# Talking-heads attention with a gated layer: value products two chunks in a run at a slot's end, and loads of q, k, v and of the first weights begun from ScalarE's queue

## The chip, the core and the metric

The kernel runs on one core of one Trainium2 chip. The metric is device time in microseconds (us), the median of several executions of one launch. TensorE (PE) multiplies into PSUM banks, with weight loads shown apart as PEld; VectorE (DVE), ScalarE (ACT) and GpSimd (POOL) do the elementwise work; transfers are begun by SyncE (SP) or by ACT, which each have a queue of their own, and are carried by 16 DMA engines that both queues share. Each engine works off its own instructions in the order in which they are written; an instruction that has to wait holds up all behind it on that engine.

## The reference, cut to what matters

```python
# 4 batches, 12 heads, 448 positions, 64 wide; 1792 tokens of 768
scores = scale * np.matmul(q, k.transpose(0, 1, 3, 2))
scores = np.einsum('bhij,hg->bgij', scores, w_pre)        # heads mixed before the softmax
scores = scores - np.max(scores, axis=-1, keepdims=True)
attn = np.exp(scores)
attn = attn / (np.sum(attn, axis=-1, keepdims=True) + 1e-09)
attn = np.einsum('bhij,hg->bgij', attn, w_post)           # and after it
attn_out = np.matmul(attn, v)
x = attn_out.transpose(0, 2, 1, 3).reshape(B * S, H * D)
gate = 1.0 / (1.0 + np.exp(-(x @ w_gate)))
out = gate * (x @ w_val) @ w_out
```

## The kernel before

The attention part works in 16 blocks of query rows (per batch 120, 120, 120 and 88 rows), cut into 180 groups of 10 rows. Ten rows times twelve heads fill the 120 partitions of one tile, so that one product mixes the heads. Slots t, one per group, set the order: the loop `for t in range(...)` writes one slot after the other, and each engine's share of a slot follows its share of the slot before.

In slot t stand, for different groups and blocks: `qk` (L163, L164), the scores of one head of the block after next or so, which `keep` copies to a tile `st` (L172 on ACT for odd heads, L174 on DVE for even ones); `premix(t + 4)` (L203), the first mix of heads, from the tile `T` into one of two PSUM banks `pm`; `rowmax(t + 4)` (L210, DVE); `p_lo(t + 1)` (L248, DVE) and `scale(t + 2)` (L233, POOL); `mix(t - 1)` (L266, ACT); what the plan holds for the slot (loads, splits of k and q on POOL, `av`); `expo(t + 4)` (L219, ACT), which frees a `pm` bank; the slot's share of the second part (`moe.slot`); and `postmix(t)` (L260), the second mix, twelve short products `mx`.

`regroup(t)` (L198) moves ten rows of `st` to one of five tiles `T`, from SP, written up to seven slots ahead; it waits until `premix` of five groups earlier has read that tile, and, for the first group of a block, until all twelve heads of the block are in `st`. There are two tiles `st`, so the first copy of a block into `st` waits until the last `T` of the block before the last has landed.

`av(bi, c)` (L280) multiplies values: chunk c of six of block bi is 16 short products. After chunk 3 and after chunk 5 ACT copies the result (`xt`, L288) and begins its store (`xs`, L289). The six chunks of a block were spread over the slots of the next block by `at(spread(c, KC, s0, s1), av, bi, c)`.

All loads are written by `nc.sync.dma_start`, in the slots that `fit(loads)` gives them: 18 of k (L122, 448 KB each), 15 of q (L140, 528 or 720 KB), 12 of v (L181, 512 KB). They stand on SP between the transfers of `T`. The second part (`_Moe`) has a plan of its own, made ahead of time; its weights are loaded raw (L839, 768 KB each), turned into float32 on ACT and DVE (L848, L852, L857), stored (L861) and loaded again (L864); its first weights and the rows of x (L872) are loaded in the last slots of the attention.

The DMAs of the two queues take eight semaphores, named DMAHW0 to DMAHW7 in the listings below, in turn: each DMA first waits for the landing of the one written eight DMAs before it, where that is not yet known.

Of the kernel before, what the change touches and what calls it, by code (L numbers as in the profile page):

```python
# [14 lines left out]
I8 = mybir.dt.int8  # L15
# [19 lines left out]
def _attention(ctx, tc, ins, B, H, S, D, xs, raws, make_moe):  # L35

    nc = tc.nc
    qd, qp, kd, kp, vb = (ins[n] for n in ("qd", "qp", "kd", "kp", "vb"))
# [3 lines left out]
    KC = H * D // 128  # L42
# [29 lines left out]
    def bank(pool, tag):  # L72
        return pool.tile([128, 512], F32, tag=tag, name=tag)
# [35 lines left out]
    NG = len(groups)  # L109
    moe = make_moe(NG)  # L110
# [8 lines left out]

    def k_load(b, c):  # L120
        t = kld[len(kraw) % len(kld)]
        nc.sync.dma_start(out=t, in_=kd[b, c])  # L122
        kraw[b, c] = t

    def k_split(b, c, e):
# [10 lines left out]
    def q_load(bi):  # L136

        b, i0, n, _ = blocks[bi]
        t = qld.tile([128, H * QB], F32, tag="qd", name="qd")
        nc.sync.dma_start(out=t[:, :H * n], in_=qd[b, :, H * i0:H * (i0 + n)])  # L140
        qraw[bi] = t[:, :H * n].rearrange("p (h s) -> p h s", s=n)

    def q_split(bi, u):
# [34 lines left out]

    def v_load(b, u):
        t = vst.tile([128, QUAD, 4, D], F32, tag="v", name="v")  # L180
        nc.sync.dma_start(out=t.rearrange("p h j d -> p (h j d)"), in_=vb[b, u])  # L181
        vt[b, u] = t


# [6 lines left out]
    def pairs(t):  # L191

        return kind[t]

    def regroup(t):
        _, bi, r0 = groups[t]
        T = tp.tile([KR, S], F32, tag="T", name="T")
        nc.sync.dma_start(out=T, in_=st_t[bi][r0:r0 + R])  # L198
        t_t[t] = T

    def premix(t):
        ps = bank(ps_pm, "pm")
        nc.tensor.matmul(ps[:, :S], lhsT=w1, rhs=t_t.pop(t), start=True, stop=True)  # L203
        sc_t[t] = ps

    def rowmax(t):

        nm = sm.tile([128, 1], F32, tag="nm", name="nm")
        junk = jp.tile([128, S], F16, tag="junk", name="junk")
        nc.vector.tensor_scalar(junk, sc_t[t][:, :S], -SCALE, None, op0=ALU.mult, op1=ALU.min,  # L210
                                accum_out=nm)
        nm_t[t] = nm

    def expo(t):
        e = ep.tile([128, S], F32, tag="e", name="e")
        if t % 2 == 0:
            ss_p[0] = sm.tile([128, 2], F32, tag="ss", name="ss")
        ss = ss_p[0][:, t % 2:t % 2 + 1]
        nc.scalar.activation(out=e, in_=sc_t.pop(t)[:, :S], func=AF.Exp, bias=nm_t.pop(t),  # L219
                             scale=SCALE, accum_out=ss)  # L220
        e_t[t], ss_t[t] = e, ss

    def norm():
        nc.vector.tensor_scalar(ss_p[0], ss_p[0], 1e-9, 1.0 / P_UP, op0=ALU.add, op1=ALU.mult)

    def recip():
        nc.vector.reciprocal(ss_p[0], ss_p[0])

    def scale(t):

        if pairs(t):
            ph = pp.tile([128, S], F16, tag="ph", name="ph")
            nc.gpsimd.tensor_scalar(ph, e_t[t], ss_t[t], 1.0, op0=ALU.mult, op1=ALU.mult)  # L233
            p_t[t] = [ph]
            if pairs(t) == 2:
                e, pl = e_t.pop(t), pp.tile([128, S], F16, tag="pl", name="pl")
                nc.gpsimd.tensor_scalar(e, e, ss_t.pop(t), 1.0, op0=ALU.mult, op1=ALU.mult)
                nc.gpsimd.tensor_tensor(pl, e, ph, op=ALU.subtract)
                p_t[t].append(pl)
        else:  # L240
            w = wp.tile([128, H * R], F32, tag="w2s", name="w2s")
            nc.gpsimd.tensor_scalar(w, w2, ss_t.pop(t), 1.0, op0=ALU.mult, op1=ALU.mult)
            p_t[t] = w

    def p_lo(t):
        if pairs(t) == 1:
            pl = pp.tile([128, S], F16, tag="pl", name="pl")
            nc.vector.scalar_tensor_tensor(pl, e_t.pop(t), ss_t.pop(t), p_t[t][0], op0=ALU.mult, op1=ALU.subtract)  # L248
            p_t[t].append(pl)

    def postmix(t):
        ps = bank(ps_mx, "mx")[:, :4 * H * R].rearrange("p (j c) -> p j c", j=4)
        if pairs(t):
            ph, pl = p_t.pop(t)
            terms = [(ph, w2hi), (ph, w2lo), (pl, w2hi)]
        else:
            terms = [(e_t.pop(t), p_t.pop(t))]
        for jb in range(4):
            for i, (a, w) in enumerate(terms):
                nc.tensor.matmul(ps[:, jb, :], lhsT=a[:, JB[jb]:JB[jb] + 128], rhs=w,  # L260
                                 start=(i == 0), stop=(i == len(terms) - 1))
        mx_t[t] = ps

    def mix(t):
        _, bi, r0 = groups[t]
        nc.scalar.activation(out=mixes[bi % 2][:, :, :, r0:r0 + R],  # L266
                             in_=mx_t.pop(t).rearrange("p j (g r) -> p j g r", r=R), func=AF.Copy, scale=fm)
# [25 lines left out]
    SOFT = 4  # L293
# [5 lines left out]
    def at(slot, fn, *args):  # L299
        plan.setdefault(slot, []).append((fn, args))  # L300

    def spread(i, n, s0, s1):
        return s0 + i * (s1 - s0) // n
# [38 lines left out]
    for bi in range(1, NBK):  # L342
        s0, s1 = qwin[bi]
        for g in range(H):
            at(spread(g, H, s0, s1), qk, bi, g)
        for u in range(NQ):
            due = spread(u * QUAD, H, s0, s1) - 2
            if bi > 1:
                splits.append((due - 4 if u else due - 2, due, q_split, bi, u))
        if bi > 1:  # L350
            loads.append((max(s0 - 12, -5), max(s0 - 8, -1), q_load, bi))
    fit(loads)
    fit(splits, lambda slot: slot % 4)
    for bi in range(NBK):
        s0 = first[bi + 1] + 1
        s1 = first[bi + 2] + 1 if bi + 2 < len(first) else s0
        for c in range(KC):
            at(spread(c, KC, s0, s1), av, bi, c)
            if bi == NBK - 1:
                at(s1, moe.between, c)  # L360

# [25 lines left out]
    def qk_first(g, pool, tag):  # L387
        n = blocks[0][2]
        c, e = divmod(g, 2)
        sc = bank(pool, tag)  # L390
        nc.tensor.matmul(sc[:n, :S], lhsT=qraw[0][HI[e], c], rhs=kone[0, c][HI[e]], start=True, stop=True)
        return sc
# [13 lines left out]
    for c in range(1, NP):  # L406
        k_first(c)
    mix_in = load_mix()
    q_load(1)
    hb = bank(ps_av, "av")  # L410
    warm(10)
# [3 lines left out]
    todo = [qk_first(g, *pools[g]) for g in range(AHEAD)]  # L415
# [18 lines left out]
    for t in range(min(min(plan), -LEAD), max(plan) + 1):  # L434
        while next_dma < min(NG, t + LEAD + 1) and t >= qwin[groups[next_dma][1]][1]:
            regroup(next_dma)
            next_dma += 1
        todo = plan.get(t, ())
        for fn, args in todo:
            if fn is qk:  # L440
                fn(*args)
        if 0 <= t + SOFT < NG:
            premix(t + SOFT)
            rowmax(t + SOFT)
        sums = t % 2 == 0 and 0 <= t + PREP < NG + 1
        if sums:
            norm()
        if 0 <= t + 1 < NG:
            p_lo(t + 1)
        if sums:  # L450
            recip()
        if 0 <= t + 2 < NG:
            scale(t + 2)
        for c in hooks.get(t, ()):
            c.close()
        if 0 <= t - 1 < NG:
            mix(t - 1)
        for fn, args in todo:
            if fn is not qk:
                fn(*args)  # L460
        if 0 <= t + SOFT < NG:
            expo(t + SOFT)
        if t == NG:
            nc.scalar.activation(out=iw, in_=sw, func=AF.Sigmoid)
        moe.slot(t)
        if 0 <= t < NG:
            postmix(t)
    return moe


# [19 lines left out]
class _Moe:  # L490
# [345 lines left out]

    def load_raw(self, k):

        self.nc.sync.dma_start(out=self.at["raw", k].bitcast(I8)[:, :8 * self.WE - 3], in_=self.src[k].bitcast(I8)[:, 3:])  # L839

    def top(self, k, step):

# [77 lines left out]

    def slot(self, t):
        a = t - self.NG
        if a == self.ROOM[0][0]:
            self.open(0)
        if a == self.ROOM[1][0]:
            self.open(1)
        if a == 0:
            self.open(2)
        if a == -3:
            self.open_banks(5, side="right")  # L930
        self.until(min(self.SLOT * (a + 1), 3.4) if a else 3.4)
# [98 lines left out]
```

## Time and profile before

| | |
|---|---|
| median of 3 runs | 1010.58 us (1008.87 to 1017.09) |
| the profiled execution, its own time | 1007.51 us |
| its span, first to last instruction | 1005.6 us |
| attention, about | 0 to 510 us of the span |
| PE busy | 939.6 us (93%) |
| DVE, ACT, POOL busy | 696.9, 613.1, 275.7 us |
| mean granted TensorE clock | 0.981 of full speed |
| chain that ended last | PE 63%, DMA 17%, ACT 11%, DVE 5% |
| bytes moved by the DMA engines | 144.48 MB |

A row of a timeline gives the start in us from the span's start, the duration in us, the engine (with a q where only its queue is at work), line, operation and tiles; in square brackets stands how long the engine had been idle before, and what ended that.

### The profile page before, as it was taken

The page shows a single profiled execution, that of the slowest core. Times are in us where ns is not written, and L with a number is a line of the kernel's source. Part 1 is how long each engine was busy: PE and PEld are TensorE (multiplying, and loading weights), DVE is VectorE, ACT ScalarE, POOL GpSimd, SP SyncE. Part 2 cuts the span into 40 slices and gives each one's busy share as a digit, 9 for nine tenths or more (in the row PEclk, how much of TensorE's full clock was granted, in tenths as well). Part 3 has the DMA queues.
Part 4 walks back from the last instruction along what each step waited for, and adds up shares of the span by engine and source line. Part 5 has one row for each costly group of instructions (what it writes and reads, how often), then busy time and mean ns, then how long its engine had stood idle before and what let it go on. Part 6 is the DMA issues. An engine that isn't in the chain of part 4 may idle for free.

```text
span 1005.6 us, 17847 instructions
## 1 busy us (share of the span) xinstructions
PE 939.6 (93%) x6606; PEld 749.7 (75%) x6606; DVE 696.9 (69%) x1243; ACT 613.1 (61%) x1061; POOL 275.7 (27%) x354
## 2 busy tenths in 40 slices
PE   7889999899989999979789999999899999999998
PEld 2656676566766677656568888888699999999997
DVE  7556777578665667645468877788988766669882
ACT  3555667566665666667596888799455444446460
POOL 6246755478546864422210000000000000000000
PEclk8899999999999999999999999999899999999999
DMA  5666567665677665766825555778644321210002
GB/s 162 158 165 171 133 129 190 156 169 114 146 195 173 139 125 118 176 164 133 237 90 185 192 189 188 250 242 292 207 146 166 94 63 52 75 48 1 28 10 74
DMA packets 71333, 144.48 MB, mean 144 GB/s; under 512 B 18167, under 2 KB 49999, under 8 KB 71247
## 3 DMA queue, kind: packets, MB, share of 16 engines
q1 hardware_dynamic: 58024, 137.63, 50.0%
q10 hardware_dynamic: 13223, 5.70, 2.1%
q8 instruction: 53, 0.87, 0.3%
q14 instruction: 33, 0.27, 0.1%
HBM read 79.44 MB, written 25.17 MB: 104 GB/s over the span
## 4 chain that ended last, share of the span: by engine, by line
PE 63%; DMA 17%; ACT 11%; DVE 5%; issue 3%; SPq 1%; ACTq 0%; DVEq 0%
PE bank L888 18%; DMA T<-st 13%; PE bank L899 13%; PE pm L203 11%; PE mx L260 9%; PE av L280 6%; DMA raws<-in_w_dram 4%; ACT raws L852 4%; PE qk L163 3%; ACT m_GV L875 3%; PE qk L164 2%; ACT raws L848 2%; ACT m_FWTR L905 1%; DVE st L174 1%; DVE m_FWTR L881 1%
## 5 line engine op out<-in xcount | busy, mean ns | idle before, releaser
L888 PE MATMUL bank<-m_GV 128*128 128x448 f32 x1512 | 314.2, 368 | 10.8 <-ACT m_FWTR L905 5.2
L888 PEld LDWEIGHTS bank<-m_GV 128*128 128x128 f32 x1512 | 284.1, 189 | 40.0 <-ACT m_FWTR L905 7.8
L210 DVE TENSOR_SCALAR_CACHE_REDUCE junk<-pm 128x448 f16<-128x448 f32 x180 | 112.0, 622 | 132.5 <-PE pm L203 129.1
L203 PE MATMUL pm<-T,w 120*128 120x448 f32 x360 | 173.2, 563 | 28.7 <-DMA T<-st 19.8
L219 ACT ACTIVATE e<-pm,nm 128x448 f32<-128x448 f32 x180 | 114.3, 635 | 124.7 <-DVE junk L210 71.9
L878 DVE TENSOR_TENSOR m_GV<-m_FWTR,m_GV 128x768 fp32r<-128x768 f32 (+1 forms) x137 | 154.4, 1138 | 49.9 <-ACT m_GV L875 47.9
L875 ACT CAST m_GV<-m_FWTR 128x768 fp32r<-128x768 f32 (+1 forms) x137 | 134.9, 1001 | 56.7 <-DVE m_FWTR L881 28.3
L899 PE MATMUL bank<-m_GV 128*128 128x448 f32 x756 | 158.9, 371 | 6.5 <-ACT m_GV L875 3.9
L899 PEld LDWEIGHTS bank<-m_GV 128*128 128x128 f32 x756 | 143.8, 191 | 21.2 <-ACT m_GV L875 4.7
L233 POOL TENSOR_SCALAR ph<-e,ss 128x448 f16<-128x448 f32 x151 | 98.5, 660 | 156.4 <-ACT e L219 94.8
L260 PEld LDWEIGHTS <-ph 128*128 128x128 f16 x1208 | 91.6, 98 | 47.4 <-issue 38.7
L248 DVE SCALAR_TENSOR_TENSOR pl<-e,ss,ph 128x448 f16<-128x448 f32 x151 | 122.2, 809 | 4.1 <-POOL ph L233 3.8
L266 ACT ACTIVATE mix<-mx,fm 128x480 f32<-128x480 f32 x180 | 121.2, 673 | 2.5 <-PE mx L260 2.5
L280 PEld LDWEIGHTS av<-mix,v 128*64 128x64 f32 x1504 | 73.6, 138 | 59.1 <-issue 40.5
L260 PE MATMUL mx<-w2hi,pl 128*128 128x120 f16 x604 | 105.2, 217 | 9.5 <-DVE pl L248 9.5
L260 PE MATMUL mx<-w2hi,ph 128*128 128x120 f16 x604 | 106.3, 219 | 1.5 <-POOL qhh L149 0.6
L260 PE MATMUL mx<-w2lo,ph 128*128 128x120 f16 x604 | 105.3, 217 | 0.0
L203 PEld LDWEIGHTS pm<-T,w 120*128 120x128 f32 x360 | 66.4, 194 | 46.7 <-ACT mix L266 15.7
L280 PE MATMUL av<-mix,v 128*64 128x120 f32 (+1 forms) x1504 | 93.5, 268 | 0.0
L905 ACT COPY m_FWTR<-bank 128x448 f32<-128x448 f32 x96 | 52.8, 554 | 60.4 <-PE bank L888 45.4
L163 PE MATMUL qk<-kT,qhh 128*120 128x448 f32 (+1 forms) x180 | 80.1, 445 | 2.4 <-POOL qhh L149 1.9
L174 DVE COPY st<-qk 120x448 f32<-120x448 f32 (+1 forms) x92 | 56.3, 613 | 35.4 <-PE qk L164 14.6
(70 smaller groups left out, 1041.6 us busy)
## 6 DMA issues: line engine op xcount, KB each, us to landing
T<-st SPq DMA_DIRECT2D x180, 210.0 KB
raws<-in_w_dram SPq DMA_DIRECT2D x36, 767.6 KB
w<-m_FWTR SPq DMA_DIRECT2D x36, 384.0 KB
m_FWTR<-w SPq DMA_DIRECT2D x31, 384.0 KB
raws<-in_kd_dram SPq DMA_DIRECT2D x18, 448.0 KB
qd<-in_qd_dram SPq DMA_DIRECT2D x11, 720.0 KB
raws<-w SPq DMA_DIRECT2D x17, 384.0 KB
v<-in_vb_dram SPq DMA_DIRECT2D x12, 512.0 KB
```

What stands on the lines that cost most here:

```text
L163: nc.tensor.matmul(sc[:n, :S], lhsT=hh[:, h, :n], rhs=kt, start=True, stop=False)
L203: nc.tensor.matmul(ps[:, :S], lhsT=w1, rhs=t_t.pop(t), start=True, stop=True)
L210: nc.vector.tensor_scalar(junk, sc_t[t][:, :S], -SCALE, None, op0=ALU.mult, op1=ALU.min, accum_out=nm)
L219: nc.scalar.activation(out=e, in_=sc_t.pop(t)[:, :S], func=AF.Exp, bias=nm_t.pop(t), scale=SCALE, accum_out=ss)
L248: nc.vector.scalar_tensor_tensor(pl, e_t.pop(t), ss_t.pop(t), p_t[t][0], op0=ALU.mult, op1=ALU.subtract)
L260: nc.tensor.matmul(ps[:, jb, :], lhsT=a[:, JB[jb]:JB[jb] + 128], rhs=w, start=(i == 0), stop=(i == len(terms) - 1))
L266: nc.scalar.activation(out=mixes[bi % 2][:, :, :, r0:r0 + R], in_=mx_t.pop(t).rearrange("p j (g r) -> p j g r", r=R), func=AF.Copy, scale=fm)
L280: nc.tensor.matmul(av_t[bi][64 * i:64 * i + 64, c % 4, :n], lhsT=vt[b, u][:, h + i, jb, :], rhs=mixes[bi % 2][:, jb, 2 * c + i, :n], start ...
L875: self.nc.scalar.copy(self.f32(hi).bitcast(F32R), self.f32(f))
L878: self.nc.vector.tensor_tensor(self.f32(lo).bitcast(F32R), self.f32(f), self.f32(hi), op=ALU.subtract)
L888: self.nc.tensor.matmul(self.f32(bank), lhsT=w[a][:, k], rhs=x[b][:, k], start=self.START[i] and k == r == 0, stop=k == self.KH - 1 and r ...
L899: self.nc.tensor.matmul(self.f32(bank), lhsT=w[a][:, k], rhs=b[bb], start=self.START[i] and j == k == r == 0, stop=j == OUT_TILES - 1 and ...
```

## The change

The loads of k, q and v go from SP's to ACT's queue, and so do raw weight loads up to seven slots before the last group. In a slot `premix` and `rowmax` now stand ahead of `qk`. The chunks of `av` fall due in pairs (chunks 0 and 1, 2 and 3, 4 and 5 in the same slot, every fourth slot of a block of twelve), and they stand at the slot's end, behind `postmix`, with the copy and the store of their result. The last block's six chunks stay together behind the last group.

```diff
     def k_load(b, c):
-        nc.sync.dma_start(out=t, in_=kd[b, c])
+        nc.scalar.dma_start(out=t, in_=kd[b, c])
     def q_load(bi):
-        nc.sync.dma_start(out=t[:, :H * n], in_=qd[b, :, H * i0:H * (i0 + n)])
+        nc.scalar.dma_start(out=t[:, :H * n], in_=qd[b, :, H * i0:H * (i0 + n)])
     def v_load(b, u):
-        nc.sync.dma_start(out=t.rearrange("p h j d -> p (h j d)"), in_=vb[b, u])
+        nc.scalar.dma_start(out=t.rearrange("p h j d -> p (h j d)"), in_=vb[b, u])
...
-            at(spread(c, KC, s0, s1), av, bi, c)
+            at(spread(c - c % 2, KC, s0, s1), av, bi, c)
...
+        if 0 <= t + SOFT < NG:
+            premix(t + SOFT)
+            rowmax(t + SOFT)
         for fn, args in todo:
             if fn is qk:
                 fn(*args)
-        if 0 <= t + SOFT < NG:
-            premix(t + SOFT)
-            rowmax(t + SOFT)
...
+        tail = (av, moe.between)
         for fn, args in todo:
-            if fn is not qk:
+            if fn is not qk and fn not in tail:
                 fn(*args)
         if 0 <= t + SOFT < NG:
             expo(t + SOFT)
+        if t >= NG:
+            for fn, args in todo:
+                if fn in tail:
+                    fn(*args)
...
         if 0 <= t < NG:
             postmix(t)
+            for fn, args in todo:
+                if fn in tail:
+                    fn(*args)
...
     def load_raw(self, k):
-        self.nc.sync.dma_start(...)
+        self.loads.dma_start(...)
...
     def slot(self, t):
         a = t - self.NG
+        self.loads = self.nc.scalar if a < -7 else self.nc.sync
```

On SP, in the first block's slots, the transfers of `T` stood between loads of k (`raws<-in_kd_dram`), q and v before the change:

```order
L198 DMA T<-st 120x1x448 x8
L122 DMA raws<-in_kd_dram 128x896
L198 DMA T<-st 120x1x448
L122 DMA raws<-in_kd_dram 128x896
L198 DMA T<-st 120x1x448
L140 DMA qd<-in_qd_dram 128x1056
L198 DMA T<-st 120x1x448
L181 DMA v<-in_vb_dram 128x1024
L198 DMA T<-st 120x1x448
```

After the change 173 transfers of `T` stand on SP without a load between them, and only the loads of x (`m_FWTR<-xs`, now L880) still stand between the last seven:

```order
L375 DMA mix_132<-in_kp_dram 128x448 x5
L198 DMA T<-st 120x1x448 x173
L880 DMA m_FWTR<-xs 128x3x224 x2
L198 DMA T<-st 120x1x448
L880 DMA m_FWTR<-xs 128x3x224 x2
```

On ACT those loads (49 of them in the slots and ahead of them: 15 of q, 18 of k, 12 of v, 4 of weights) now stand between `mix` and `expo` of a slot; here with what each instruction waits for, in the first block's slots:

```order
L266 ACTIVATE mix_131<-mx,fm 128x48x10
L122 DMA raws<-in_kd_dram 128x896 [waits DMAHW2_49]
L219 ACTIVATE e,ss<-pm,nm 128x448 [waits DVE_49,Activation_49]
L266 ACTIVATE mix_131<-mx,fm 128x48x10 [waits PE_49]
L140 DMA qd<-in_qd_dram 128x1056 [waits DMAHW5_49,Pool_49]
L219 ACTIVATE e,ss<-pm,nm 128x448 [waits DVE_49,Activation_49]
```

A load on ACT waits for one of the eight DMA semaphores, and one of q for POOL as well; the exponentials stand behind it.

On PE a slot with one chunk of `av` read so before the change (an `av` row of x8 is one chunk):

```order
L260 MATMUL mx<-w2hi,pl 128x120
L163 MATMUL qk<-kT,qhh 88x448
L164 MATMUL qk<-kT,qll 88x448
L203 MATMUL pm<-T,w_121 128x448
L280 MATMUL av<-mix_132,v 64x120 x8
L260 LDWEIGHTS ph
L260 MATMUL mx<-w2hi,ph 128x120
```

and after it two chunks stand behind the slot's `mx`, with `premix` of the next slot behind them:

```order
L260 MATMUL mx<-w2hi,pl 128x120
L280 MATMUL av<-mix_131,v 64x120 x16
L203 MATMUL pm<-T,w_121 128x448
L163 MATMUL qk<-kT,qhh 88x448
L164 MATMUL qk<-kT,qll 88x448
L260 LDWEIGHTS ph
L260 MATMUL mx<-w2hi,ph 128x120
```

## Rows read from the trace of the kernel before

**Rows 1.** The view of windows: the four stretches of the attention in which most loads run. Columns: start and end; length, then busy us and number of instructions of each engine; granted clock of PE, mean busy share of the DMA engines, GB/s.

```profile
27.00:110.00 83.00, 74.33 (x569) 51.83 (x570) 47.01 (x128) 47.05 (x112) 45.06 (x63) 0.96 0.68 166
155.00:215.00 60.00, 54.19 (x531) 36.77 (x530) 39.07 (x99) 34.75 (x80) 35.69 (x47) 0.97 0.72 177
280.00:335.00 55.00, 48.12 (x481) 32.46 (x480) 32.55 (x91) 32.01 (x75) 32.58 (x43) 1.00 0.72 175
397.00:450.00 53.00, 46.18 (x439) 30.70 (x436) 30.93 (x85) 34.20 (x73) 20.33 (x28) 0.97 0.69 166
```

**Rows 2.** The same view: the three stretches between them, with few loads.

```profile
110.00:155.00 45.00, 44.01 (x452) 31.61 (x451) 33.53 (x83) 30.04 (x68) 26.36 (x35) 1.00 0.60 122
215.00:280.00 65.00, 64.63 (x649) 45.81 (x647) 48.20 (x118) 43.65 (x100) 43.99 (x55) 1.00 0.63 139
335.00:397.00 62.00, 60.99 (x628) 43.77 (x627) 41.83 (x111) 40.35 (x91) 40.94 (x51) 1.00 0.60 127
```

**Rows 3.** The view of waits: who waited for whom; us in total, times, longest.

```profile
PE pm L203 <- DMA T<-st: 19.8, 18, 2.4
PE mx L260 <- DVE pl L248: 9.5, 6, 3.5
DVE st L174 <- DMA T<-st: 12.5, 3, 6.7
```

**Rows 4.** The timeline of SP's queue in the first stretch with loads (a row of several transfers ends with the last issue).

```profile
47.65 2.79 SPq L198 DMA_DIRECT2D T<-st  x1
50.50 0.50 SPq L122 DMA_DIRECT2D raws<-in_kd_dram  x1
51.10 2.98 SPq L198 DMA_DIRECT2D T<-st  x1
...
54.72 3.67 SPq L198 DMA_DIRECT2D T<-st  x2
```

**Rows 5.** The timeline of PE there: the product that waited for the `T` begun at 47.65.

```profile
55.40 0.99 PE L203 MATMUL pm<-T,w 120*128 120x448 f32 x2 [1.11 <-DMA T<-st]
```

**Rows 6.** The timelines of SP's queue and of PE at the start: the first `T`, with no load near it, and the product that waited for it.

```profile
13.95 4.28 SPq L198 DMA_DIRECT2D T<-st  x3
...
19.44 1.11 PE L203 MATMUL pm<-T,w 120*128 120x448 f32 x1 [1.89 <-DMA T<-st]
```

**Rows 7.** The timelines of DVE and PE around 80 us, where a copy to `st` came late.

```profile
79.71 0.62 DVE L174 COPY st<-qk 88x448 f32<-88x448 f32 x1 [3.00 <-PE pm L203]
...
81.52 0.28 PE L260 MATMUL mx<-w2hi,pl 128*128 128x120 f16 x1 [2.23 <-DVE pl L248]
...
82.47 0.66 PE L163 MATMUL qk<-kT,qhh 128*88 128x448 f32 x1
```

**Rows 8.** The timeline of PE between 127 and 157 us, without the twelve `mx` of each slot: slots with and without a chunk of `av` of 120 and of 88 columns.

```profile
127.49 0.92 PE L203 MATMUL pm<-T,w 120*128 120x448 f32 x2
...
128.85 0.44 PE L163 MATMUL qk<-kT,qhh 128*120 128x448 f32 x1
...
129.34 0.92 PE L203 MATMUL pm<-T,w 120*128 120x448 f32 x2
...
132.26 0.92 PE L203 MATMUL pm<-T,w 120*128 120x448 f32 x2
...
152.41 0.92 PE L203 MATMUL pm<-T,w 120*128 120x448 f32 x2
153.26 0.83 PE L280 MATMUL av<-mix,v 128*64 128x88 f32 x16
...
155.12 0.92 PE L203 MATMUL pm<-T,w 120*128 120x448 f32 x2
```

**Rows 9.** The timeline of PE behind the last group, where the last block's six chunks (88 columns, 16 instructions each) stand in a run: four chunks in one bank, two in another.

```profile
512.18 2.65 PE L280 MATMUL av<-mix,v 128*64 128x88 f32 x64
514.66 1.38 PE L280 MATMUL mx<-mix,v 128*64 128x88 f32 x32
```

**Rows 10.** The views of single lines: of the loads of v on SP and of the stores on ACT, the shortest, median and longest issue in ns.

```profile
L181 SPq DMA_DIRECT2D v<-in_vb_dram x12: 487/1423/2843, 47.0 to 422.5; - x12
L289 ACTq DMA_DIRECT2D xs<-xt x30: 366/366/400, 86.6 to 508.6; - x30
```

**Rows 11.** The timeline of ACT around one store, and around the third raw weight tile's first step.

```profile
95.88 0.38 ACTq L289 DMA_DIRECT2D xs<-xt  x1
96.37 0.64 ACT L219 ACTIVATE e<-pm,nm 128x448 f32<-128x448 f32 x1 [0.52 <-DVE pl L248]
...
449.95 0.67 ACT L266 ACTIVATE mix<-mx,fm 128x480 f32<-128x480 f32 x1
...
454.67 0.92 ACT L848 ACTIVATE raws<-raws 128x768 int32<-128x768 int8 x1
```

**Rows 12.** SP's issue of that weight tile, and one load of raw weights in the chain of work that ended last, behind the attention, where no `T` runs (start, us, what).

```profile
443.40 0.49 SPq L839 DMA_DIRECT2D raws<-in_w_dram  x1
...
559.21 4.71 DMA raws<-in_w_dram
```

**Rows 13.** The timeline of DVE in the slot that begins at 127.4 us: `rowmax` and the next group's `p_lo`; and from the page's costliest groups that of all `p_lo` (count, busy us, mean ns, idle time before it and its releaser).

```profile
128.44 0.62 DVE L210 TENSOR_SCALAR_CACHE_REDUCE junk<-pm 128x448 f16<-128x448 f32 x1
...
129.07 1.64 DVE L248 SCALAR_TENSOR_TENSOR pl<-e,ss,ph 128x448 f16<-128x448 f32 x1
...
L248 DVE SCALAR_TENSOR_TENSOR pl<-e,ss,ph 128x448 f16<-128x448 f32 x151 | 122.2, 809 | 4.1 <-POOL ph L233 3.8
```

More of the change, by code (lines that the diff above doesn't have):

```diff
@@ L837, in load_raw @@
     def load_raw(self, k):
-        self.nc.sync.dma_start(out=self.at["raw", k].bitcast(I8)[:, :8 * self.WE - 3], in_=self.src[k].bitcast(I8)[:, 3:])
+        self.loads.dma_start(out=self.at["raw", k].bitcast(I8)[:, :8 * self.WE - 3], in_=self.src[k].bitcast(I8)[:, 3:])
     def top(self, k, step):
```

## The prediction

> **What bounds the kernel now.** I read the view of windows first. In the stretches with few loads PE is nearly without idle time: 44.01 of 45, 64.63 of 65 and 60.99 of 62 us busy at full clock, 2.4 us idle in 172 [rows 2]. There a slot lasts as long as PE's work, 1.85 us without a chunk of `av` (127.49 to 129.34) and 2.92 with one (129.34 to 132.26), a mean of about 2.4 [rows 8]. In the four stretches with loads PE idles 8.67 + 5.81 + 6.88 + 6.82 = 28.2 of 251 us, and in three of them the granted clock falls to 0.96 or 0.97, which is another 0.04 x 83 + 0.03 x 60 + 0.03 x 53 = 6.7 us of work [rows 1]; the reader is to see that all other engines have more idle time there than PE. Then the view of waits: `premix` waited for `T` 19.8 us, `mx` for `p_lo` 9.5 us, and the copies to `st` for the landing of `T` 12.5 us [rows 3]. The last two are one thing: at 79.71 the copy had held DVE up for 3.00 us, `p_lo` behind it came late, PE stood for 2.23 us at 81.52, and its next `qk` took 0.66, where one at full clock took 0.44 [rows 7, 8]. So most of what PE loses in the attention is `T` that comes late.
>
> Why late: SP's queue. Where loads stand between the `T`, a `T` is begun every 3.45 to 3.62 us (47.65, 51.10, 54.72), for its own issue lasts 2.8 to 3.0 us and the load's 0.5 [rows 4], while a slot needs one per 2.4 us. They also travel longer: begun at 47.65 and waited for until 55.40, 7.75 us [rows 4, 5], against 5.5 us for the first `T` (13.95 to 19.44) [rows 6].
>
> **Loads to ACT's queue: what it takes away.** SP keeps only `T`: each load slot loses an issue of 0.5 us and its gap, and `T` no longer stands behind a whole load's packets. A slot's lateness grew by 3.5 - 2.4 = 1.1 us; with the 2.8 to 3.0 us of a crowded `T` left it would still grow by up to 0.6, with an uncrowded one by nothing. Bounds: from 0 (the engines that carry both are the limit) to all idle time above what the quiet stretches show, 28.2 - 251 x 2.4/172 = 24.7, and the clock's 6.7, together 31 us. I take 60%, 18 us: the growth falls from 1.1 to between 0 and 0.6, but some tail remains, since each `T` now also waits for a load eight DMAs earlier, which ACT begins some slots later than SP did, and the loads of x stay on SP.
>
> The Trainium skill, DMA: Bandwidth & Descriptors, section Issuing engines are not separate DMA queues, speaks against this term: DMAs begun from several engines run on the same 16 DMA engines, and only issue time is saved. By that alone the 18 waits for `T` would each lose one load's issue, some 0.6 us, 11 us in all, for 990 us by an estimate. The same page, Queues, rings and completion order, says that a DMA engine goes round its queues packet by packet, which would let `T` pass a load in another queue; no row of this trace has both queues loaded with long transfers.
>
> **What ACT pays.** 49 loads. On ACT a store's issue lasts 0.366 us in all 30 cases, though SP is often held up at the time [rows 10]; from its start to the next instruction's, 95.88 to 96.37, go 0.49 us [rows 11]. 49 x 0.5 = 24 us of ACT, covered by ACT's idle third (busy 30.04 of 45, 43.65 of 65 us) [rows 2]. Behind a load stands `expo(t + 4)`, which frees the `pm` bank for `premix(t + 6)` and feeds POOL and DVE. If the cover were gone the 24 us would all count. I take +2.
>
> The raw weight tiles: SP began the third at 443.40 for a step on ACT at 454.67 [rows 11, 12]. From ACT it is begun two exponentials ahead of that step, by the rows of before about 450, behind the `mix` of 449.95. 4.7 us is what such a load takes without `T` beside it (559.21) [rows 12], 7.75 what `T` took among loads [rows 4, 5]. So ACT waits between 0 and 3.1 us for this one, less for the two before it, which have a slot more. Bounds 0 to 9, I take +2. At the very start the first q load goes beside the first k loads; DVE, not they, sets the pace, so 0, at most one pair of rows 4, 3.5.
>
> **Two chunks in a run.** A chunk alone adds 2.92 - 1.85 = 1.07 us to a slot (120 columns), or 2.71 - 1.85 = 0.86 (88 columns, 152.41 to 155.12) [rows 8]. Behind the last group four 88-column chunks take 514.66 - 512.18 = 2.48 us, 0.62 each [rows 9]. A second chunk directly behind the first so saves 0.86 - 0.62 = 0.24; for 120 columns, with 0.62 x 120/88 = 0.845, 0.22. 15 blocks have three pairs: 33 x 0.22 + 12 x 0.24 = 10.1 us where PE sets the pace. Bounds: 0 (PE would have waited anyway) to 10. I take 10, since PE is at 98% in the quiet stretches. The first chunk's place behind `mx` instead of behind `pm` I cost at nothing: both are followed by a weight load for another shape.
>
> **`premix` ahead of `qk`.** The same instructions, so 0 on PE; but `T` is wanted earlier by the two `qk` products ahead of it, 0.5 us (128.85 to 129.34 [rows 8]), and `st` is written that much later. In the quiet stretches nothing waits for `T`, so that is covered; in the loaded ones it is in the 40% that I leave. The work behind the chunks: ACT's copy of the result now waits at the end of a slot, with the next slot's `mix` behind it, which is not wanted before that slot's end.
>
> Sum against the profiled execution's own time: 1007.5 - 18 - 10 + 2 + 2 = 983.5 us. That execution lay 3 us under the median of the runs shown; the forecast for the median is 985.
>
> **The rivals.**
> Only the run of chunks pays. If the DMA engines themselves are the limit where loads run (their mean share is 0.68 to 0.72 there, 0.60 to 0.63 elsewhere [rows 1, 2]), `T` is as late as before: 1007.5 - 10 + 4 = 1001 to 1002. For it: `T`'s longer journey among loads. Against it: 28 to 32% of the engines' time is unused. This is the case that the page's sentence on issue time leans to.
>
> ACT becomes the bound, and it is slower. If a load's issue on ACT is held up as v's on SP is (median 1.42, longest 2.84 us [rows 10]), ACT, which has 0.33 x 2.4 = 0.8 us to spare in a slot, is late by 1.42 + 0.1 - 0.8 = 0.7 us per load, 35 us, and with the 28 gained this gives 1015; at 2.84 us it is 105 us, and 1084. From 1.5 us per issue on it is slower by over 1%. Against it: the 30 stores that never took more than 0.4 us.
>
> Short slots in a run. Before, a slot of 1.85 us stood beside one of 2.92 [rows 8]; now three short ones follow each other, then one of 1.85 + 1.9. `p_lo(t + 1)` must be done when `mx(t + 1)` starts, now 1.85 + 0.85 (`pm`, 152.41 to 153.26) + 0.5 (`qk`) = 3.2 us after slot t's start. DVE's `rowmax` began 0.95 us after its `pm` (127.49, 128.44); it takes 0.62, a copy to `st` 0.62 and `p_lo` 0.81 on the mean, 3.0 together; with the longest shown, 1.64, it is 3.8 [rows 7, 8, 13]. So the margin is 0.2 us, and the exponential that frees a bank has one like it. If three of four slots lose 0.15 us on the mean, 135 x 0.15 = 20 us, the sum is 1004. Against it: DVE is busy 33.53 of 45 us where PE sets the pace [rows 2], so a late `p_lo` is caught up in the long slot.
>
> **How the numbers follow.** Forecast (the waits for `T` mostly go, 970 to 997): 0.57. Only the run of chunks: 0.20. Short slots: 0.13. ACT the bound: 0.10. The predicted time is that of the first, 985. The range, 966 to 1006, reaches from nearly the full 31 and 10 us (1007.5 - 41 + 0 = 966) over the second and third case, and leaves out the fourth and the mishaps below. A measurement of this kernel can tell about 1% from no change. Faster by over 1% (under 1000.5): nearly all of the first case and a third of the second and third, 0.64; within 1%: 0.28; slower: the rest of the fourth, 0.08.
>
> **What would show it.** SP's issues of `T` about 2.4 us apart in the stretches of rows 1, PE's idle time there near 10 instead of 28 us, and the wait of `st` for `T` gone: the first term. A slot with two chunks of 120 columns 1.85 + 1.9 us long, other slots 1.85: the second. Issues of loads on ACT of 0.3 to 0.5 us: the third; issues over 1.4 us would make the prediction wrong, and so would waits of PE for `p_lo` or for `expo` in the quiet stretches, which have none now, or a journey of `T` of over 8 us with the loads gone from SP.

## The result, and the profile after

The changed kernel took 984.88 us (983.05 to 984.97, 4 runs) beside 1013.19 (1008.87 to 1017.09) for the kernel before: ratio 0.972, 95% interval 0.967 to 0.977. Measured again beside three of the experiments it took 988.19 us, ratio 0.9785 (0.976 to 0.981). So the change is worth 2.2 to 2.8%, 22 to 29 us; the forecast was 985. The profiled execution took 983.05 us, its span 981.0. Most of the sum came out, but two of its terms did not come from where I had put them.

The view of windows, with the borders moved so that each stretch holds the same groups as in [rows 1]:

```profile
26.00:104.00 78.00, 73.90 (x585) 53.34 (x587) 49.46 (x133) 48.42 (x116) 46.85 (x64) 0.96 0.69 175
...
148.00:202.00 54.00, 51.06 (x515) 35.47 (x514) 40.25 (x97) 33.73 (x80) 35.93 (x46) 1.00 0.74 203
...
266.00:317.00 51.00, 47.86 (x485) 32.92 (x483) 36.38 (x91) 31.85 (x78) 32.77 (x42) 1.00 0.74 204
...
377.00:425.00 48.00, 44.85 (x465) 31.33 (x464) 32.26 (x85) 34.22 (x74) 21.32 (x30) 1.00 0.70 178
```

The loaded stretches shrank from 251 to 231 us and PE's idle time in them from 28.2 to 13.3. The quiet ones, in the same view:

```profile
104.00:148.00 44.00, 43.09 (x455) 30.91 (x451) 33.78 (x80) 27.76 (x66) 26.61 (x34) 1.00 0.59 125
...
202.00:266.00 64.00, 63.91 (x649) 45.28 (x647) 49.50 (x120) 40.98 (x98) 45.22 (x55) 1.00 0.60 128
...
317.00:377.00 60.00, 59.65 (x615) 42.57 (x613) 45.02 (x113) 37.88 (x89) 39.19 (x48) 1.00 0.58 125
```

They went from 172 to 168 us only [rows 2]. Of the 24 us that these seven stretches lost, 20 came from where loads run.

The view of waits of the changed kernel (who waited for whom; us in total, times, longest), beside [rows 3]:

```profile
PE pm L203 <- DMA T<-st: 12.4, 7, 3.4
PE pm L203 <- ACT e L219: 10.9, 14, 2.0
...
PE mx L260 <- ACT mix L266: 3.5, 4, 1.3
PE mx L260 <- DVE pl L248: 2.7, 5, 1.2
...
DVE st L174 <- DMA T<-st: 0.3, 1, 0.3
```

`pm` waits 7 times for `T` instead of 18, and what is left stands, but for 1.21 us, at the first block and in the last groups, where the loads of x still share SP's queue. New is the second row: `pm` waits for the exponential, 10.9 us where it was 3.8. The timeline of SP's queue in the first loaded stretch, single rows:

```profile
45.10 2.52 SPq L198 DMA_DIRECT2D T<-st  x1
...
47.72 2.60 SPq L198 DMA_DIRECT2D T<-st  x1
...
50.43 2.32 SPq L198 DMA_DIRECT2D T<-st  x1
```

A `T` is begun every 2.6 to 2.7 us, where it was 3.45 to 3.62 [rows 4]. In this stretch one issue still takes 2.3 to 2.6 us, but no load follows it; over all 180 of them SP's issue of a `T` fell from 1.58 to 0.97 us at the median.

The journey of a `T` did not get shorter. The `T` of the fifteenth group is the one of [rows 4, 5], begun at 47.65 and waited for until 55.40. In the changed kernel it was begun at 43.28; the view of the chain there (start, us, what) shows how long it took to land, and PE's row that its product then waited for something else:

```profile
43.28 10.10 DMA T<-st
```

```profile
54.62 0.64 PE L203 MATMUL pm<-T,w 120*128 120x448 f32 x1 [1.07 <-ACT e L219]
```

Its tile is free when the tenth group's product, five groups earlier, has read it. That product began at 41.36 before and at 41.67 after, so this `T` was begun 6.3 us behind it before and 1.6 us after. It travelled 10.10 us where it had taken 7.75 at most, and came in time because it was begun earlier. Among the products that stood for their `T`, the longest journey was 9.08 us before (178.70 to 187.78) and 11.57 in the second profile of loads alone, a run of the next section (391.37 to 402.94).

The issues on ACT, by the views of the lines of the loads of k, q, v and raw weights (shortest, median, longest, ns):

```profile
L122 ACTq DMA_DIRECT2D raws<-in_kd_dram x18: 334/522/2657, 37.8 to 303.1; - x18
L140 ACTq DMA_DIRECT2D qd<-in_qd_dram x15: 334/339/452, 2.3 to 378.0; - x15
L181 ACTq DMA_DIRECT2D v<-in_vb_dram x12: 334/338/2665, 45.1 to 402.6; - x12
L847 ACTq DMA_DIRECT2D raws<-in_w_dram x4: 334/352/353, 399.2 to 459.1; - x4
```

By the medians that is the 0.3 to 0.5 us of the prediction. But the issue is not all that a load costs ACT. The view of the chain around 160 us shows what the load of v there was waiting for (start, us, what):

```profile
153.73 7.95 DMA T<-st
161.69 0.02 issue
161.71 0.34 ACTq L181
```

and the timeline of ACT, then the row of PE, show who stood behind it:

```profile
158.84 0.68 ACT L266 ACTIVATE mix<-mx,fm 128x480 f32<-128x480 f32 x1
161.71 0.34 ACTq L181 DMA_DIRECT2D v<-in_vb_dram  x1
162.15 0.64 ACT L219 ACTIVATE e<-pm,nm 128x448 f32<-128x448 f32 x1 [2.63 <-DMA T<-st]
```

```profile
162.92 0.64 PE L203 MATMUL pm<-T,w 120*128 120x448 f32 x1 [2.04 <-ACT e L219]
```

The load had to wait until a `T` begun at 153.73 had landed; ACT works in order, so ACT stood 2.63 us ahead of the exponential and PE 2.04 us for its bank. The queue that the load left no longer waits for it, and the engine that took it over now waits for `T`.

Last, two chunks in a run, in the timeline of PE (the products `mx` and `qk` left out):

```profile
129.61 0.97 PE L203 MATMUL pm<-T,w 120*128 120x448 f32 x2
...
131.57 1.86 PE L280 MATMUL av<-mix,v 128*64 128x120 f32 x32
133.36 1.02 PE L203 MATMUL pm<-T,w 120*128 120x448 f32 x2
...
135.27 0.97 PE L203 MATMUL pm<-T,w 120*128 120x448 f32 x2
...
137.13 0.60 PE L203 MATMUL pm<-T,w 120*128 120x448 f32 x1
```

The slot with two chunks is 3.75 us long (forecast 1.85 + 1.9), the slot without 1.86, and the slot right behind the run 1.91. Two chunks with one short slot cost 5.61 us, against 5.84 for two slots of 2.92 before [rows 8].

### The profile page after: what moved, and what is told of

The parts are those of the page before. It is cut to its first block, busy times and chain, and to the rows that moved or that the text cites. A ratio compares the mean times of both kernels' runs of the same rounds, so it can differ in the third digit from the quotient of the medians.

```text
span 981.0 us, 17817 instructions
## 1 busy us (share of the span) xinstructions
PE 924.9 (94%) x6606; PEld 748.8 (76%) x6606; DVE 710.3 (72%) x1243; ACT 605.4 (62%) x1061; POOL 276.3 (28%) x354
## 2 busy tenths in 40 slices
DMA packets 71333, 144.48 MB, mean 147 GB/s; under 512 B 18167, under 2 KB 49999, under 8 KB 71247
## 3 DMA queue, kind: packets, MB, share of 16 engines
q10 hardware_dynamic: 20279, 33.67, 11.1%
## 4 chain that ended last, share of the span: by engine, by line
PE 63%; ACT 12%; DMA 11%; DVE 8%; issue 3%; POOL 2%; ACTq 0%; SPq 0%; POOLq 0%; DVEq 0%
PE bank L896 18%; PE bank L907 13%; PE pm L203 11%; PE mx L260 8%; PE av L280 7%; DMA raws<-in_w_dram 5%; DMA T<-st 4%; ACT raws L860 4%; ACT m_GV L883 3%; PE qk L163 2%; PE qk L164 2%; ACT raws L856 2%; DVE pl L248 2%; DVE junk L210 1%; ACT e L219 1%
## 5 line engine op out<-in xcount | busy, mean ns | idle before, releaser
L203 PE MATMUL pm<-T,w 120*128 120x448 f32 x360 | 181.0, 585 | 23.4 <-DMA T<-st 12.4
L248 DVE SCALAR_TENSOR_TENSOR pl<-e,ss,ph 128x448 f16<-128x448 f32 x151 | 130.1, 862 | 12.3 <-POOL ph L233 12.3
L163 PE MATMUL qk<-kT,qhh 128*120 128x448 f32 (+1 forms) x180 | 126.2, 701 | 0.4 <-POOL qhh L149 0.4
L260 PEld LDWEIGHTS <-ph 128*128 128x128 f16 x1208 | 85.7, 98 | 37.2 <-issue 27.0
L172 ACT COPY st<-qk 120x448 f32<-120x448 f32 (+1 forms) x92 | 49.0, 533 | 90.9 <-PE qk L164 87.7
L280 PE MATMUL av<-mix,v 128*64 128x120 f32 (+1 forms) x1504 | 83.5, 265 | 0.0
L203 PEld LDWEIGHTS pm<-T,w 120*128 120x128 f32 x360 | 55.4, 193 | 34.7 <-ACT e L219 13.4
L916 DVE TENSOR_TENSOR m_FWTR<-bank,m_FWTR 128x448 f32<-128x448 f32 x90 | 55.6, 621 | 35.3 <-PE bank L907 19.8
```

Source lines behind the costliest of these rows:

```text
L163: nc.tensor.matmul(sc[:n, :S], lhsT=hh[:, h, :n], rhs=kt, start=True, stop=False)
L280: nc.tensor.matmul(av_t[bi][64 * i:64 * i + 64, c % 4, :n], lhsT=vt[b, u][:, h + i, jb, :], rhs=mixes[bi % 2][:, jb, 2 * c + i, :n], start ...
```

## The experiments

All ratios are against the kernel before, measured beside each. For the attention I give the same groups each time (27 to 450 us before, 26 to 425 after), as length and PE's busy time; idle is the difference.

**Each part alone.** Loads alone: the three `dma_start` of k, q and v, and that of raw weights up to group NG - 8.

```
-        nc.sync.dma_start(out=t, in_=kd[b, c])
+        nc.scalar.dma_start(out=t, in_=kd[b, c])
```

> The kernel before with the loads of q, k, v and of the early raw weights begun from ACT's queue, and nothing else changed. Theory (late T, because T's issue shared SP's queue with the loads, and that is most of the gain): 14 to 18 us less than the kernel before, T begun every 2.4 to 2.7 us where loads run, PE's wait of pm for T down from 19.8 to some 5 to 8 us, the copies to st no longer held by T. Rival (the DMA engines themselves are the limit, the run of chunks pays alone): 0 to 4 us, T as late as before. By the Trainium skill (DMA: Bandwidth & Descriptors, Issuing engines are not separate DMA queues) alone, an estimate: only the loads' issue time goes, 11 us less.

Measured 987.42 us, ratio 0.9754 (0.973 to 0.978). All other parts, with the loads back on SP:

> The changed kernel with all loads back on SP's queue: two chunks in a run at a slot's end, and premix ahead of qk, remain. Theory (each part pays for itself, 18 and 10 us): 8 to 10 us less than the kernel before, T late as before (wait of pm for T near 20 us, st held by T). Rival (only the run of chunks pays): 25 to 28 us less, all of the gain. Second rival (the parts need each other: with T late, PE stands anyway, and what the run saves is lost there): 0 to 4 us.

Measured 1007.96 us, 0.9975 (0.995 to 1.000). The order alone (the two lines of `premix` and `rowmax` moved ahead of `qk`):

> The kernel before with premix and rowmax ahead of qk in each slot, and nothing else changed. Theory (same instructions, T wanted 0.5 us earlier): within 3 us of the kernel before, if anything slower, since T is late there and st is written later. Rival (rowmax 0.5 us earlier gives DVE and ACT room, and the waits of mx for p_lo, 9.5 us, go): 4 to 9 us less.

Measured 1006.62, 0.9956 (0.994 to 0.997). The run alone, in the chunks' old place:

```
-            at(spread(c, KC, s0, s1), av, bi, c)
+            at(spread(c - c % 2, KC, s0, s1), av, bi, c)
```

> The kernel before with two chunks of av in a run, in their old place between premix and mx in the middle of a slot; nothing else changed. Theory (a second chunk directly behind the first saves 0.22 to 0.24 us, 45 times, wherever the run stands): 8 to 10 us less, as much as with the run at a slot's end. Rival (the place matters: in the middle of a slot the run of 1.9 us holds up mx, and with it mix, while the next pm comes late): 0 to 4 us less, or slower; pm and the exponential then wait.

Measured 1005.49, 0.9938 (0.992 to 0.996). That is 6 us, between the theory and the rival. The order alone gave some 4 us, just beyond the theory; its profile does not show where, since the same groups took 424 us there and 423 before.

So the loads alone give 25 us, as much as the whole change, and all the rest without them 2.5. Both the theory (18 and 10) and the rival that only the run pays fall. In the kernel with the rest alone `pm` waited 31.7 us for `T`, 12 more than before: PE did its work faster and stood longer.

**With the loads on ACT.** What are the other parts then worth? The changed kernel again, with `qk` first again, with one chunk in a slot again, and with the loads behind the exponential:

> The changed kernel once more, unaltered, beside the three below: 25 to 30 us less than the kernel before.

> The changed kernel with qk ahead of premix and rowmax again, as in the kernel before; loads on ACT and the run of chunks at the slot's end stay. Theory (with T early the order is worth nothing): within 3 us of the changed kernel. Rival (rowmax and the exponential begin 0.5 us earlier in a slot with premix first; that order alone took 4.5 us off the kernel before): 3 to 6 us more than the changed kernel, with longer waits of pm for the exponential and of mx for p_lo.

> The changed kernel with each chunk of av in a slot of its own again, but still at the slot's end; loads on ACT and premix first stay. Theory as predicted (the run of chunks saves 0.22 to 0.24 us 45 times, and shows in the time once PE is not kept waiting by T): 8 to 10 us more than the changed kernel, av's busy time up by 8 to 10 us. Theory after the first four runs (loads alone gave 25 of the 28 us, so what the run saves is mostly lost in other waits): av's busy time up as much, the time by 2 to 4 us only, PE's idle time smaller than in the changed kernel.

```
+        behind = (k_load, q_load, v_load)
...
-            if fn is not qk and fn not in tail:
+            if fn is not qk and fn not in tail + behind:
                 fn(*args)
         if 0 <= t + SOFT < NG:
             expo(t + SOFT)
+        for fn, args in todo:
+            if fn in behind:
+                fn(*args)
```

> The changed kernel with the loads of q, k and v begun on ACT behind the slot's last exponential instead of ahead of it. Theory (a load on ACT waits for the landing of a T eight DMAs earlier, and holds up the exponential behind it, as from 159.5 to 161.7 in the changed kernel, and PE then waits for a bank: 10.9 us of pm waiting for the exponential in all): the exponential is no longer behind it, 5 to 8 of the 10.9 us go, 4 to 7 us less than the changed kernel. Rival (ACT stands as long, and the copy to st or the mix of the next slot is late instead): within 2 us of the changed kernel, waits of mx or qk for ACT in the place of those of pm.

Measured: unaltered 0.9785 (0.976 to 0.981); `qk` first 0.9775 (0.975 to 0.980); one chunk in a slot 0.986 (0.983 to 0.989); loads behind the exponential 0.977 (0.974 to 0.980). The order makes no difference with `T` early. Loads behind the exponential cut `pm`'s waits for it from 9.4 to 1.8 us, but `T` and `mix` took 6.5 us more; the time is the same, as the rival had it.

One chunk in a slot cost 7 us, which looked like the run's worth. Only a part of it can be: its attention up to 428 us took 401 us, that of the changed kernel 399 and 397 in its two profiles. The rest was lost behind that. The last value product of the attention began at 505.8 us, in the changed kernel at 492.8 and 491.0. PE's longest stop there stands in ACT's timeline and PE's row:

```profile
467.70 0.36 ACT L288 COPY xt<-av 128x240 f32<-128x240 f32 x1 [0.21 <-PE av L280]
475.07 0.37 ACTq L289 DMA_DIRECT2D xs<-xt  x1
475.49 0.67 ACT L266 ACTIVATE mix<-mx,fm 128x480 f32<-128x480 f32 x1 [7.43 <-DMA T<-st]
```

```profile
476.30 0.54 PE L260 MATMUL mx<-w2s,e 128*128 128x120 f32 x1 [4.59 <-ACT mix L266]
```

A store on ACT stood 7 us for a `T`, and PE 4.59 us for the `mix` behind it; from 475 to 480 us the granted clock was 0.50, the lower of its two levels, where it had been 1.00 from 470 to 472.5. It is the same mechanism as at 161.71: a transfer's wait on ACT's queue holds up ACT's own work. What the run at the slot's end would be worth without such a stop is not shown.

**Loads alone against loads and run.** The comparison with one difference:

> The kernel before with only the loads on ACT's queue once more, beside the next three: 22 to 27 us less than the kernel before, and within 3 us of the changed kernel measured elsewhere, if the other parts of the change give nothing together.

> The kernel before with the loads on ACT's queue and two chunks of av in a run in their old place in the middle of a slot; premix stays behind qk. Theory (a run saves 10 us of PE's work, and the changed kernel loses it again by its place at the slot's end and premix ahead of qk): 7 to 11 us less than with the loads alone, and faster than the changed kernel. Rival (what a run saves turns into waits wherever it stands, since the other slots get short): within 3 us of the loads alone, PE's busy time down by 8 to 10 us and its idle time up by as much.

> The kernel of the run before this one, with the loads of q, k and v begun behind the slot's last exponential on ACT. Theory (the stall of a load for an earlier DMA no longer holds up the exponential; in the changed kernel that edit took pm's waits for the exponential from 9.4 to 1.8 us but gave T and mix 6.5 us more): within 3 us of the run before this one. Rival (with premix behind qk the saved waits count): 4 to 7 us less.

Measured: loads alone 0.972 (0.969 to 0.976), with the run in the old place 0.973 (0.970 to 0.976), and with the loads behind the exponential as well 0.972 (0.969 to 0.975). The same groups in the view of windows, loads alone:

```profile
28.00:424.00 396.00, 387.34 (x3739) 273.32 (x3737) 276.44 (x713) 261.32 (x594) 248.25 (x316) 0.99 0.67 163
```

and loads and run:

```profile
28.00:424.00 396.00, 379.79 (x3753) 276.24 (x3752) 281.90 (x712) 257.05 (x593) 247.00 (x316) 0.99 0.67 163
```

The run takes 7.6 us off PE's work and puts as much idle time in its place: 8.7 us idle became 16.2. In the first profile of loads alone the same groups took 401 us with PE busy for 386.67, 14.3 idle, so one execution of this kernel differs from another by as much; what stands is PE's saving of 7 us, and a time that is the same within the intervals (some 4 us). Where the idle time of these two profiles lies, the view of waits shows; loads alone:

```profile
PE pm L203 <- ACT e L219: 3.7, 6, 1.8
PE mx L260 <- ACT mix L266: 2.0, 3, 1.2
```

loads and run:

```profile
PE pm L203 <- ACT e L219: 6.7, 8, 1.8
PE mx L260 <- ACT mix L266: 6.1, 5, 1.8
PE pm L203 <- ACT mix L266: 3.3, 2, 1.8
```

and with the loads behind the exponential:

```profile
PE mx L260 <- ACT mix L266: 12.4, 12, 1.8
...
PE pm L203 <- ACT e L219: 1.9, 2, 1.3
```

PE's waits for ACT in these rows go from 5.7 to 16.1 us with the run, and from 16.1 to 14.3 when the loads are moved in the slot: the stall mostly stays and changes its victim. (In the first profile of loads alone the two rows were 9.5 and 1.6 us, 11.1 in all, so how much of the idle time the run brings differs between executions; the move from one row to the other was seen in the changed kernel too, above.)

**Another queue.** The changed kernel with the same loads begun from POOL's queue (`nc.gpsimd.dma_start`):

> The changed kernel with the same loads begun from POOL's queue in place of ACT's. Theory (what the loads cost is their place on SP ahead of T, not the queue that they go to; POOL is busy 28% of the span): 20 to 30 us less than the kernel before, with ACT no longer standing for an earlier DMA and pm's waits for the exponential below 4 us. Rival (a load costs POOL much more than 0.5 us, or holds up the splits and products behind it there): p_lo and ph come late, and it is 5 us or more slower than the changed kernel.

Measured 1012.67 us, 1.002 (0.999 to 1.004): the whole gain is gone, which neither expected. ACT no longer stood for a load, as the theory said (`pm`'s wait for the exponential was 0.4 us), and a load took POOL 0.58 to 0.60 us, the first one 0.72. But `pm` waited 31.7 us for `T`, and `mx` 13.1 us for `mix`: ACT now stood 18.4 us, in four places, until a store had landed and the next result could be copied. The rows of the view of waits, and the longest of those places in ACT's timeline:

```profile
PE pm L203 <- DMA T<-st: 31.7, 18, 6.1
PE mx L260 <- ACT mix L266: 13.1, 6, 4.8
```

```profile
298.92 0.30 ACT L288 COPY xt<-av 128x176 f32<-128x176 f32 x1 [8.69 <-DMA xs<-xt]
```

Rows of SP's queue, of PE and of the view of windows for one late `T`:

```profile
45.18 1.88 SPq L198 DMA_DIRECT2D T<-st  x1
```

```profile
58.93 1.09 PE L203 MATMUL pm<-T,w 120*128 120x448 f32 x1 [4.40 <-DMA T<-st]
```

```profile
50.00:55.00 5.00, 4.24 (x24) 3.13 (x22) 2.44 (x7) 3.09 (x8) 3.91 (x7) 1.00 0.95 271
```

This `T` is that of the fifteenth group again. It was begun as early as with the loads on ACT, 1.6 us behind the tenth group's product (43.58), but took 13.75 us until its product began, where it had landed after 10.10. A `T` can be begun at most five groups ahead; at 2.4 us a slot that is 12 us (an estimate from [rows 8]), which covers the one journey and not the other. POOL had begun the six loads from the third one on within 11.0 us (42.32 to 53.35), and the mean share of the DMA engines was 0.95 from 50 to 55 us. In the changed kernel ACT began the same six within 15.6 us (37.79 to 53.40), and the share there was 0.81. So getting out of SP's queue is not enough. On ACT loads wait, among others for a `T` to land, which spaces them; on POOL they followed each other faster. That the spacing decides is argued from these rows and not shown: POOL's loads also went through a queue that the page lists as another kind (software_dynamic) and in fewer packets (70,182 in all, not 71,333), and spaced loads on POOL were not run.

## Why the prediction was right, step by step

**Loads to ACT's queue, 18 us: right on the beginning of `T`, wrong on its journey, too small.** By the ratios of loads alone it is 25 to 28 us, what ACT pays already taken off, where my sum had 18 - 2 - 2 = 14; that is near the upper bound of 31. `T`'s spacing fell to 2.6 or 2.7 us (forecast about 2.4), and with loads alone PE idled 8.7 or 14.3 us in the attention, against 30.6 before. The 40% that I left for a tail (loads that `T` waits for, x on SP) was mostly not there: from 27 to 440 us `pm` waited about 2 us for `T`. The step that failed is that a `T` "no longer stands behind a whole load's packets" and so travels faster: it travelled longer, 10.10 us. A journey of over 8 us was to make the prediction wrong; it came, and the gain came all the same, since the earlier beginning covers it. Of the 6.7 us that the clock was to give back, 3 stayed: the granted clock of the first stretch is 0.96 as before. One sign I misread: with loads alone the copies to `st` still waited 11.2 us for `T` (12.5 before), and PE 3.8 for `st` and 4.5 for `p_lo` (9.5 before); the wait of `st` went only with the full change. So the waits of `st` and `p_lo` are not one thing, as I had read them; in [rows 7] the copy at 79.71 waited for `pm` by its own row, not for `T`. The Trainium skill, DMA: Bandwidth & Descriptors, section Issuing engines are not separate DMA queues, says that only the time to begin a transfer is saved. The trace agrees: this `T` was begun 4.7 us earlier behind its tile's last reader and travelled no faster. What was too small is my estimate of 11 us from it, which counted one load's issue for each of 18 waits and left out that SP's issues of `T` get shorter too. The same section's statement that all queues run on the same DMA engines agrees with the run on POOL, where this `T` travelled longer beside closer loads.

**Two chunks in a run, 10 us: right on PE, wrong in time.** `av` fell from 93.5 to 83.5 us of PE's busy time, and a pair is as long as computed. (The 15 blocks hold 36 pairs of 120 columns and 9 of 88, not 33 and 12; the sum stays 10.1 us.) The step that failed is the cover: I took the upper bound because "PE is at 98% in the quiet stretches", but those are 172 of 423 us, so some 18 of the 45 pairs, 4 us, lie there. In the loaded stretches the saving became waits, for `T` with the loads on SP, for ACT with the loads on ACT. With the loads moved the run in its old place was worth nothing measurable (0.973 against 0.972); in the kernel before it was worth 6 us alone, and at the slot's end one chunk in a slot was 7 us slower, of which 2 to 4 us lie in the attention up to 428 us.

**What ACT pays, 2 us: too small.** The issues were as cheap as forecast, and ACT did not become the bound. But I counted only issue time. The wait of a load for an earlier transfer stood in the order of instructions, and on an engine with its own work it holds up all that follows: `pm` waited 6 to 7 us more for the exponential. What is left of the loads' gain after it is in the 25 to 28 us. I had named the other direction of this wait alone (a `T` behind a load).

**Order and place, 0: too small on PE.** For the same groups PE's busy time is 379.8 us with the run in the old place (377.4 with the loads behind the exponential as well), 384.3 and 382.8 in two profiles of the changed kernel (383.2 with its loads behind the exponential), and 385.7 with the run at the slot's end but `qk` first. So the place at the slot's end costs PE 3 to 6 us; a part of it is seen in the slot behind a run (1.91 against 1.86 us), and the cause is open. In the time it can't be told from nothing.

**Raw weight tiles, 2 us.** ACT's wait for them rose from 8.7 to 12.2 us, within the bounds; it was not tried by itself.

So 985 came out because the loads, with what ACT pays, gave 11 to 14 us more than the sum had, and the run with its place some 10 less. That the two errors cancel is luck. Of the rivals, short slots in a run was nearest: its sign was right (late exponentials and mixes), its cause (`p_lo`) not, since `mx` waited 2.7 us for `p_lo`, 9.5 before.

## What to carry to other kernels

Keep loads out of the queue that feeds the critical path: moving 49 transfers to ACT's queue, with no other edit, gave the whole gain here. When you move a transfer, move its wait in your sum too: on an engine that computes, all work behind it waits, and look at how closely transfers follow each other in the queue that it goes to. A saving on the busiest engine counts only in the stretches where nothing else is late, so weigh it by those, and test each part alone, since two savings on one wait don't add up.

## What was not expected of the hardware

With the same loads begun from POOL in place of ACT, `T`'s issues on SP stayed short (median 0.78 us) and early, yet one `T` was waited for until 13.75 us after its issue, and the kernel was as slow as before. Nor did a `T` travel faster once the loads had left its queue for ACT's: 10.10 us to land, against 7.75 from issue to product before. And one store that waited on ACT's queue cost PE 4.59 us at once, with a granted clock of 0.50 from 475 to 480 us, at that stop's end and behind it.
